# First-layer steps in four pieces, attention slots in three parts, ordered by one time table, with the sinks a slot later

## The chip, the core and the metric

The kernel runs on one core of a Trainium2 chip. The core has a matrix engine (PE, with its weight loads listed as PEld), a vector engine (DVE), a scalar engine (ACT), a general engine (POOL) and a queue engine that only issues transfers (SP). Each takes its instructions in the order in which they were put down for it, and they wait for one another through semaphores. The metric is the device time of one execution in microseconds.

## The reference

Sliding-window attention with sink columns, over 4 batches of 8 heads, 768 positions and 64 dimensions, is followed by a two-layer network over its 3072 rows of 512 values. Of the reference this is what matters:

```python
keep = is_sink | in_window            # n_sink = 4, window = 128
scores = np.where(keep, scale * (q @ k.T), -1e9)
a = np.exp(scores - max); a = a / (a.sum(-1) + 1e-9)
x = (a @ v).transpose(0, 2, 1, 3).reshape(B * S, H * D)   # 3072 x 512
h = x @ w_in                          # 512 -> 2048
g = s * np.maximum(h, 0) ** 2 + b
out = g @ w_out                       # 2048 -> 512
```

## The kernel before

**Tiling.** The 3072 rows are eight chunks of 384 (half a batch each). A chunk's attention gives its x, transposed, as two tiles `x[0]` and `x[1]` (a rounded high part and the rest, so that a product in the fast 32-bit format keeps its accuracy). The first layer of a chunk is 16 steps (`l1_steps`, line 600). A step is 12 matmuls of 128x384 into one PSUM bank `h` (line 610): eight with `x[0]`, over the four 128-row blocks of x, then four with `x[1]`. ACT then clips and stores it to a tile `g` (line 614), and SP sends two steps' result to DRAM (`gs`, line 616). After all chunks the second layer (`second_layer`) reads `gs` back, squares it and multiplies it with the second weights in 84-matmul units (line 727). It takes the last third of the time and the change doesn't touch it.

**Attention.** Chunks 0 and 2 (`plain_slots`) have no separate sinks. The other six use `attn_slots` (line 422): a chunk is 24 units (eight heads, three blocks of 128 queries), and a unit passes through stages some slots apart.

- `unit_a` (line 314): two matmuls give the scores `sc` in a PSUM bank, DVE masks them and takes their maximum (line 331, `negm`), ACT takes the exponential `sm` (337), POOL copies the sink columns to `psk` (339).
- `unit_b`, LB = 3 slots later: PE transposes `sm` into a bank `tp` (350, 351), ACT rounds it to `hl` (355), DVE subtracts for the low part (356).
- `unit_c`, LC = 5 slots after the first: PE multiplies with the values into a bank `o` (389). At a head's last block ACT and DVE move it out (397, 398). At every fourth head PE transposes `psk` into `ts` (402), ACT and DVE make `xsk` of it (404, 405).
- `unit_d`, LD = 1 slot later, at every fourth head: for two pairs of heads PE multiplies `xsk` into `os` and `zb` (414, 416), DVE adds and scales (417, 418), ACT and POOL write the pair's `x[0]` and `x[1]` (419, 420).

Loads and the splitting of queries, keys and values (`load_pair`, `load_keys`, `load_sinks`, `prep_head`, on SP, ACT, DVE and POOL) stand some slots ahead in the table `ahead`, but never ahead of the chunk's own first slot.

**Banks.** PSUM has eight banks here: five in a pool `psA` for `sc`, `tp` and `o`, three in a pool `psO` for `h`, `ts`, `os` and `zb`.

**What sets the order.** The main loop (lines 943 to 972) writes a first-layer step of the chunk before, then as many attention slots as are due by a simple ratio: 210 slots over 112 steps, two steps ahead. So one or two whole slots follow each whole step. Each attention chunk has 24 slots that start a unit and 6 in which the last units run out; the next chunk's first slot comes behind these. Into the slots the making of second-layer weights is strewn (`early_w2`, 30 tasks, with DVE operations of up to 128x1024 at lines 227, 228 and 635). The framework then orders each engine's instructions by this order and by when it thinks that they can run.

Of the kernel before, what the change touches and what calls it, by code (L numbers as in the profile page):

```python
# [15 lines left out]
P = 128  # L16
B, H, S, D = 4, 8, 768, 64
NS = 8
BLK = 3
# [17 lines left out]
NT = B * S // TB  # L37
E0, LB0, LC0 = 9, 6, 8
ORDER = 0, 2, 1, 3, 4, 5, 6, 7
LB, LC, LD, L2, LEAD = 3, 5, 1, 2, 2  # L40


@with_exitstack
def tile_kernel(ctx, tc, qT, kT, k0, v, vsk, n_sink, window, w1, w2, s, b, out):
# [362 lines left out]
    def unit_d(k, h, i):  # L407

        if h % 4 == 3 and i == BLK - 1:
            xs = k.pairs[h // 2].xs  # L410
            for pr in (h // 2 - 1, h // 2):
                pp = k.pairs[pr]
                os_ = po("os")
                nc.tensor.matmul(os_[:, :CH], pp.vs, xs, start=True, stop=True)
                zb = po("zb")
                nc.tensor.matmul(zb[:, :CH], sels[pr % 2], xs, start=True, stop=True)
                nc.vector.tensor_tensor(out=pp.x, in0=os_[:, :CH], in1=pp.x, op=ALU.add)
                nc.vector.tensor_tensor(out=pp.x, in0=zb[:, :CH], in1=pp.x, op=ALU.mult)
                nc.scalar.copy(k.x[0][:, pr, :], pp.x)
                nc.gpsimd.tensor_tensor(out=k.x[1][:, pr, :], in0=pp.x, in1=k.x[0][:, pr, :].bitcast(F32), op=ALU.subtract)  # L420

    def attn_slots(c):
        k = new_chunk(c)
        units, ahead = [], {}
        for pr in range(H // 2):
            h, t0 = 2 * pr, 2 * BLK * pr
            units += [(h + hh, i) for hh in range(2) for i in range(BLK)]
            todo = ((-5, load_pair, pr), (-5, load_keys, h), (-2, load_sinks, pr), (-2, prep_head, h), (-2, load_keys, h + 1),
                    (1, prep_head, h + 1))
            for d, fn, a in todo:  # L430
                ahead.setdefault(max(t0 + d, 0), []).append((fn, a))
        n = len(units)

        def slot(t):
            def f():
                if t == 0:
                    make_x(k)
                for fn, a in ahead.get(t, ()):
                    fn(k, a)
                if t < n:  # L440
                    unit_a(k, *units[t])
                if 0 <= t - LB < n:
                    unit_b(k, *units[t - LB])
                if 0 <= t - LC < n:
                    unit_c(k, *units[t - LC])
                if 0 <= t - LC - LD < n:
                    unit_d(k, *units[t - LC - LD])
            return f

        return k, [slot(t) for t in range(n + LC + LD)]  # L450

    def plain_slots(c):
        k = Chunk()
# [144 lines left out]
    def l1_steps(k, before):  # L600

        tk = slice(k.c * CH, (k.c + 1) * CH)
        g = {}

        def l1(f):
            before(f)
            h = po("h")
            order = [(cc, wi, 0) for cc in range(NCC) for wi in range(2)] + [(cc, 0, 1) for cc in range(NCC)]
            for i, (cc, wi, xi) in enumerate(order):
                nc.tensor.matmul(h[:, :CH], w_in(f, wi)[:, cc * P:(cc + 1) * P], k.x[xi][:, cc, :],  # L610
                                 start=(i == 0), stop=(i == len(order) - 1))
            if f % 2 == 0:
                g[0] = kept.tile([P, 2, CH], F32, tag="g", name="g", bufs=3)
            nc.scalar.activation(g[0][:, f % 2], h[:, :CH], AF.Relu, scale=1.0 / WUP)  # L614
            if f % 2 == 1:
                nc.sync.dma_start(gs[f // 2][:, :, tk], g[0])

        return [lambda f=f: l1(f) for f in range(NF)]

    wc, raw2, T2 = {}, {}, {}  # L620
    spilled = {q: dram.tile([P, 7, 2, HD], F32R, tag=f"wd{q}", name=f"wd{q}") for q in range(EARLY, EARLY + SPILL)}
# [323 lines left out]
            weights(NP - 1, (i - 20) // 2)  # L945
    first_cm.__exit__(None, None, None)
    early = early_w2()
    n_early, n_plain, done = 5 * (EARLY + SPILL), 0, 0
    steps, slots = [], []
    for j in range(NC_):  # L950
        steps += l1_steps(k, before if j == 0 else lambda f: None)
        if j + 1 < NC_:
            k, more = (plain_slots if j == 0 else attn_slots)(ORDER[j + 1])
            slots += more
            n_plain = n_plain or len(more)
    n_last = len(steps) - NF
    i = 0
    for n in range(n_last):
        steps[n]()
        while i < len(slots) and i * n_last < (n + 1 + LEAD) * len(slots):  # L960
            slots[i]()
            i += 1
            if i == n_plain:
                scalars()
            if i > n_plain and done < n_early and (i - n_plain) * (n_early + 1) >= (done + 1) * (len(slots) - n_plain):
                next(early)()
                done += 1
        if i == len(slots):
            break
    wk_cm.__exit__(None, None, None)  # L970

    p2_cm = tc.tile_pool(name="p2", bufs=1)
# [4 lines left out]
    for m in range(n + 1, len(steps)):  # L977
        steps[m]()
        m -= n_last
# [64 lines left out]
```

## Time and profile before

| | us |
|---|---|
| median of 3 runs | 762.31 (761.02 to 762.97) |
| the profiled execution | 757.87 |
| its span, first to last instruction | 756.1 |
| first step of the first layer begins | 30.5 |
| first attention unit with sinks begins | 105.1 |
| last sinks | 461.1 |
| second layer begins | 503.5 |

The profiled execution is one run, 4.4 us below the median of the others; 1.8 us of it lie outside the span. In the profile a busy PE is not a PE at its peak, since the ends of matmuls are modelled; what counts is the start of one to the start of the next, and the idle time that the waits list.

### The profile page before, as it was taken

The numbers are of one execution on the slowest core, as the hardware profiler recorded it, in microseconds if no ns is written. First come the engines' busy times: TensorE is split into PE (matmuls) and PEld (weight loads), VectorE is DVE, ScalarE is ACT, GpSimd is POOL, SyncE is SP. The second block draws the span as 40 slices with busy tenths as digits, with TensorE's granted clock in tenths as the row PEclk, the third lists the DMA queues.
The fourth block names the chain that finished last, engine by engine and source line by source line (L and its number), as shares of the span: only waits on it lengthen the run. The fifth ranks groups of instructions, "written<-read, shape, count | busy, mean of one in ns | idle before, by whom it ended". The sixth has DMA issues, their size and how long they took to land. (4 is left out here: it accounts for less than half of the span.)

```text
span 756.1 us, 14225 instructions
## 1 busy us (share of the span) xinstructions
PE 708.1 (94%) x4852; PEld 673.9 (89%) x4852; DVE 552.2 (73%) x1367; ACT 543.1 (72%) x1253; POOL 225.3 (30%) x377
## 2 busy tenths in 40 slices
PE   8889999889899999899989989989999999999995
PEld 4678799889889899899889889989999999999995
DVE  7865655875686786795685883558888989798883
ACT  5989878768877888787887873556766576666661
POOL 4232344645544554555445551110000000000000
PEclk9999999999999999999999999999999999999998
DMA  8932254365455456354354324963353534453421
GB/s 206 374 120 85 63 179 121 117 192 205 124 164 211 132 190 209 124 169 128 101 195 129 111 71 171 331 241 113 112 150 108 163 112 142 115 164 112 151 74 60
DMA packets 63312, 114.12 MB, mean 151 GB/s; under 512 B 11520, under 2 KB 38784, under 8 KB 60416
## 3 DMA queue, kind: packets, MB, share of 16 engines
q1 hardware_dynamic: 61712, 107.43, 44.4%
q0 software_dynamic: 432, 5.51, 2.2%
q8 instruction: 40, 0.66, 0.3%
q14 instruction: 40, 0.33, 0.2%
q10 hardware_dynamic: 1088, 0.20, 0.1%
HBM read 76.16 MB, written 36.96 MB: 150 GB/s over the span
## 5 line engine op out<-in xcount | busy, mean ns | idle before, releaser
L610 PE MATMUL h<-x,w 128*128 128x384 f32 x1536 | 299.2, 343 | 3.7 <-ACT g L614 2.6
L610 PEld LDWEIGHTS h<-x,w 128*128 128x128 f32 x1536 | 265.5, 190 | 6.7 <-ACT g L614 3.8
L727 PE MATMUL Q<-v,gH 128*128 128x256 f32 x1008 | 127.8, 283 | 0.0
L727 PEld LDWEIGHTS Q<-v,gH 128*128 128x128 f32 x1008 | 124.0, 192 | 0.0
L727 PE MATMUL Q<-v,gA 128*128 128x256 f32 x756 | 99.0, 283 | 1.5 <-DVE gA L709 1.5
L698 ACT ACTIVATE gs<-gs,sbu 128x1024 f32<-128x1024 f32 x48 | 55.2, 1151 | 62.3 <-DMA gs<-gs 58.4
L727 PEld LDWEIGHTS Q<-v,gA 128*128 128x128 f32 x756 | 94.3, 192 | 1.8 <-DVE gA L709 1.7
L614 ACT ACTIVATE g<-h 128x384 f32<-128x384 f32 x128 | 62.5, 489 | 42.7 <-PE h L610 33.1
L337 ACT ACTIVATE sm<-sm,negm 128x264 f32<-128x264 f32 (+1 forms) x144 | 72.4, 503 | 21.1 <-DVE negm L331 19.7
L356 DVE TENSOR_TENSOR hl<-tp,hl 128x256 fp32r<-128x256 f32 (+1 forms) x144 | 57.3, 402 | 29.8 <-ACT hl L355 28.2
L331 DVE CUSTOM_DVE_ANT_0 sm<-sc,msk 128x264 f32<-128x264 f32 (+1 forms) x144 | 58.2, 411 | 24.9 <-PE sc L327 22.6
L306 POOL TENSOR_TENSOR kl<-kraw,kh 128x528 fp32r<-128x528 f32 (+1 forms) x48 | 62.6, 1304 | 29.3 <-ACT kh L304 24.8
L389 PE MATMUL o<-hl,vv 128*128 128x256 f32 (+1 forms) x352 | 63.1, 296 | 5.6 <-DVE hl L356 3.5
L710 ACT CAST gH<-gs 128x1024 fp32r<-128x1024 f32 x48 | 50.0, 1042 | 19.4 <-PE Q L727 10.5
L711 DVE TENSOR_TENSOR gH<-gs,gH 128x1024 fp32r<-128x1024 f32 x48 | 58.5, 1219 | 6.5 <-ACT gH L710 6.5
L708 ACT ACTIVATE gA<-gs,sbu 128x512 fp32r<-128x512 f32 x96 | 53.7, 607 | 9.5 <-PE Q L727 9.5
L339 POOL COPY psk<-sm 128x24 f32<-128x24 f32 x144 | 34.1, 241 | 86.8 <-ACT sm L337 79.6
L389 PEld LDWEIGHTS o<-hl,vv 128*128 128x128 f32 x352 | 48.6, 192 | 9.0 <-DVE hl L356 4.0
L709 DVE SCALAR_TENSOR_TENSOR gA<-gs,sbu,gA 128x512 fp32r<-128x512 f32 x96 | 54.9, 612 | 0.2 <-ACT gA L708 0.2
L355 ACT CAST hl<-tp 128x256 fp32r<-128x256 f32 (+1 forms) x144 | 49.7, 352 | 1.1 <-PE tp L351 0.6
L700 DVE SCALAR_TENSOR_TENSOR gs<-gs,sbu 128x256 f32<-128x256 f32 x48 | 23.2, 483 | 35.8 <-ACT gs L698 34.4
L326 PE MATMUL sc<-kh,qs 128*128 128x264 f32 (+1 forms) x144 | 42.0, 294 | 2.6 <-DVE negm L331 2.0
(180 smaller groups left out, 1214.4 us busy)
## 6 DMA issues: line engine op xcount, KB each, us to landing
gs<-g SPq DMA_DIRECT2D x64, 384.0 KB, 3.3
gs<-gs SPq DMA_DIRECT2D x48, 512.0 KB, 4.1
kraw<-in_kT SPq DMA_DIRECT2D x32, 264.0 KB, 2.8
wraw<-in_w SPq DMA_DIRECT2D x8, 1024.0 KB, 10.0
vraw<-in_w SPq DMA_DIRECT2D x6, 1024.0 KB, 5.3
out<-ot SPq DMA_DIRECT2D x12, 512.0 KB, 3.6
wd<-v SPq DMA_DIRECT2D x3, 1792.0 KB, 6.8
v<-wd POOLq DMA_DIRECT2D x3, 1792.0 KB, 8.9
```

Of the source, the lines that this page charges most:

```text
L306: nc.gpsimd.tensor_tensor(out=hd.kl[:, :kw], in0=hd.k[:, :kw], in1=hd.kh[:, :kw].bitcast(F32), op=ALU.subtract)
L331: nc.vector.tensor_tensor_reduce(out=sm[:, :n], in0=sc[:, :n], in1=m, scale=-0.125, scalar=BIG, op0=ALU.add, op1=ALU.min, accum_out=negm[: ...
L337: nc.scalar.activation(sm[:, :n], sm[:, :n], AF.Exp, bias=negm[:, uu], scale=-1.0, accum_out=pp.zz[:, i, hh:hh + 1])
L356: nc.vector.tensor_tensor(out=lo, in0=tp[:, a:z], in1=hi.bitcast(F32), op=ALU.subtract)
L389: nc.tensor.matmul(hd.o[:, q0:q0 + n * P], hd.vv[:, kb, :], hd.hl[:, t, c0 * P:(c0 + n) * P], start=(hd.n == 0), stop=(i == BLK - 1 and kb ...
L610: nc.tensor.matmul(h[:, :CH], w_in(f, wi)[:, cc * P:(cc + 1) * P], k.x[xi][:, cc, :], start=(i == 0), stop=(i == len(order) - 1))
L614: nc.scalar.activation(g[0][:, f % 2], h[:, :CH], AF.Relu, scale=1.0 / WUP)
L698: nc.scalar.activation(g[:, 0], g[:, 0], AF.Square, scale=root_ap)
L708: nc.scalar.activation(o[:, :, 0], x, AF.Identity, bias=b1_ap, scale=1.0)
L709: stt(out=o[:, :, 1], in0=x, scalar=b1_ap, in1=o[:, :, 0].bitcast(F32), op0=ALU.add, op1=ALU.subtract)
L711: nc.vector.tensor_tensor(out=H[:, :, 1], in0=S, in1=H[:, :, 0].bitcast(F32), op=ALU.subtract)
L727: nc.tensor.matmul(Q[j][:, rb], left[j][:, gi, rb * P:(rb + 1) * P], right[j][:, wi], start=(q == 0 and rb == 0 and i == 0), stop=(last an ...
```

## The change

A first-layer step is cut in four pieces of three matmuls (`PIECES = 4`); the bank `h` is opened by the first piece, and ACT reads it after the last. An attention slot is cut in three parts: `unit_a` with the loads and preparations, `unit_b`, and `unit_c` with `unit_d`. The six attention chunks form one row of 144 units, so that the units of one chunk follow those of the chunk before with no slots in between to run out, and loads stand ahead across the border of chunks. `LD` is 2 in place of 1. The x tiles are allocated at a chunk's first sinks and not at its first slot. The merging goes by a list of times, in steps: the plain chunk's slots end by step 14, row t of the attention stands at t2 + t dt, with t2 = 24 x 14/30 = 11.2 and dt = (112 - 2 - 11.2)/151 = 0.654 of a step, its three parts a third of dt apart; the weight tasks are spread evenly from step 16 to 110.

```diff
-LB, LC, LD, L2, LEAD = 3, 5, 1, 2, 2
+LB, LC, LD, L2, LEAD, PIECES = 3, 5, 2, 2, 2, 4
...
-    def attn_slots(c):
-        k = new_chunk(c)
+    def attn_slots(chunks):
...
+        for k in chunks:
+            for pr in range(H // 2):
+                h, t0 = 2 * pr, len(units)
+                units += [(k, h + hh, i) for hh in range(2) for i in range(BLK)]
...
-        def slot(t):
+        def part(t, j):
             def f():
...
+                if j == 0:
+                    for fn, k, a in ahead.get(t, ()):
+                        fn(k, a)
+                for fn, lag, of in ((unit_a, 0, 0), (unit_b, LB, 1), (unit_c, LC, 2), (unit_d, LC + LD, 2)):
+                    if of == j and 0 <= t - lag < n:
+                        fn(*units[t - lag])
             return f
...
+        return [[part(t, j) for j in range(3)] for t in range(n + LC + LD)]
...
-        def l1(f):
-            before(f)
-            h = po("h")
-            order = [(cc, wi, 0) for cc in range(NCC) for wi in range(2)] + [(cc, 0, 1) for cc in range(NCC)]
-            for i, (cc, wi, xi) in enumerate(order):
+        order = [(cc, wi, 0) for cc in range(NCC) for wi in range(2)] + [(cc, 0, 1) for cc in range(NCC)]
+        n = len(order) // PIECES
+
+        def l1(f, piece):
+            if piece == 0:
+                before(f)
+                g["h"] = po("h")
+            h = g["h"]
+            for i, (cc, wi, xi) in list(enumerate(order))[piece * n:(piece + 1) * n]:
                 nc.tensor.matmul(h[:, :CH], w_in(f, wi)[:, cc * P:(cc + 1) * P], k.x[xi][:, cc, :],
                                  start=(i == 0), stop=(i == len(order) - 1))
+            if piece < PIECES - 1:
+                return
...
+    chunks = [k, k2] + [new_chunk(c) for c in ORDER[2:]]
+    rows = attn_slots(chunks[2:])
+    steps = [f for j, c in enumerate(chunks) for f in l1_steps(c, before if j == 0 else lambda f: None)]
+    n_last = (NC_ - 1) * NF
+
+    t1 = (NF - LEAD) / len(plain)
+    t2 = H * BLK * t1
+    dt = (n_last - LEAD - t2) / len(rows)
+    todo = [(t * t1, f) for t, f in enumerate(plain)] + [(t2, scalars)]
+    todo += [(t2 + (t + j / 3) * dt, f) for t, row in enumerate(rows) for j, f in enumerate(row)]
+    todo += [(NF + (t + 0.5) * (n_last - LEAD - NF) / n_early, lambda: next(early)()) for t in range(n_early)]
+    todo.sort(key=lambda x: x[0])
+    n = 0
+    while todo:
+        while todo and todo[0][0] * PIECES < n + 1:
+            todo.pop(0)[1]()
         steps[n]()
+        n += 1
```

**Place 1: PE in the middle of attention.** This is PE's order in the first attention chunk before: the end of a slot, a second slot, then a whole step (`x_2` is the x of chunk 2, `w` the first weights).

```order
L350 MATMUL tp<-identr,sm 128x128
L351 MATMUL tp<-identr,sm 128x128
L389 MATMUL o<-hl,vv 128x128 x2
L389 MATMUL o<-hl,vv 128x256 x2
L326 MATMUL sc<-kh,qs 128x264
L327 MATMUL sc<-kl,qs 128x264
L350 MATMUL tp<-identr,sm 128x128
L351 MATMUL tp<-identr,sm 128x128
L610 MATMUL h<-x_2_543,w_524 128x384 x8
L610 MATMUL h<-x_2_544,w_524 128x384 x4
L326 MATMUL sc<-kh,qs 128x264
```

And this is PE's order in the same chunk now.

```order
L610 MATMUL h<-x_2_524,w_504 128x384 x3
L326 MATMUL sc<-kh,qs 128x264
L327 MATMUL sc<-kl,qs 128x264
L610 MATMUL h<-x_2_524,w_504 128x384 x2
L610 MATMUL h<-x_2_525,w_504 128x384
L350 MATMUL tp<-identr,sm 128x128
L351 MATMUL tp<-identr,sm 128x128
L610 MATMUL h<-x_2_525,w_504 128x384 x3
L389 MATMUL o<-hl,vv 128x128 x2
L389 MATMUL o<-hl,vv 128x256 x2
L610 MATMUL h<-x_2_524,w_546 128x384 x3
```

Three matmuls of the first layer now stand between scores, transposes and products, where twelve stood behind two whole slots.

**Place 2: PE from the sinks' transposes to the sinks' products.** Before, at the end of the chunk's first half:

```order
L402 MATMUL ts<-identr,psk_102 128x128 x3
L610 MATMUL h<-x_2_543,w_665 128x384 x8
L610 MATMUL h<-x_2_544,w_665 128x384 x4
L326 MATMUL sc<-kh,qs 128x264
L327 MATMUL sc<-kl,qs 128x264
L350 MATMUL tp<-identr,sm 128x128
L351 MATMUL tp<-identr,sm 128x128
L414 MATMUL os<-xsk,vs 128x384
```

Now, at the same heads, from the second piece on (a piece of three and one pair of scores stand between `ts` and these rows):

```order
L610 MATMUL h<-x_2_524,w_631 128x384 x3
L350 MATMUL tp<-identr,sm 128x128
L351 MATMUL tp<-identr,sm 128x128
L610 MATMUL h<-x_2_524,w_631 128x384 x2
L610 MATMUL h<-x_2_525,w_631 128x384
L326 MATMUL sc<-kh,qs 128x264
L327 MATMUL sc<-kl,qs 128x264
L610 MATMUL h<-x_2_525,w_631 128x384 x3
L350 MATMUL tp<-identr,sm 128x128
L351 MATMUL tp<-identr,sm 128x128
L610 MATMUL h<-x_2_524,w_631 128x384 x3
L389 MATMUL o<-hl,vv 128x256 x2
```

The product of the sinks follows two matmuls later. Between the transposes and it there are 15 matmuls of the first layer, two pairs of scores, two pairs of transposes and four products, where there were 12, one pair and one pair.

**Place 3: PE at the first border of attention chunks.** These rows are the chunk's last sinks now, up to the first matmul of the next chunk's first layer (its x is `x_1`).

```order
L416 MATMUL os<-xsk,vs 128x384
L418 MATMUL zb<-xsk,sel_100 128x384
...
L416 MATMUL os<-xsk,vs 128x384
...
L418 MATMUL zb<-xsk,sel_101 128x384
L610 MATMUL h<-x_2_525,w_1032 128x384
L389 MATMUL o<-hl,vv 128x128 x2
L389 MATMUL o<-hl,vv 128x256 x2
L610 MATMUL h<-x_2_525,w_1032 128x384 x3
L326 MATMUL sc<-kh,qs 128x264
L327 MATMUL sc<-kl,qs 128x264
L610 MATMUL h<-x_1_1738,w_470 128x384 x3
```

Before, two whole steps stood between these sinks and that matmul; now it is the rest of one.

## Rows read from the trace of the kernel before

**Rows 1.** The page, its first part: busy time, share of the span and instructions of each engine.

```profile
PE 708.1 (94%) x4852; PEld 673.9 (89%) x4852; DVE 552.2 (73%) x1367; ACT 543.1 (72%) x1253; POOL 225.3 (30%) x377
```

**Rows 2.** Busy time in three stretches (attention beside the first layer; the rest of the first layer; the second layer): length, then busy us and count of PE, PEld, DVE, ACT and POOL, the granted clock, the DMA share and GB/s.

```profile
105.00:462.00 357.00, 333.17 (x2140) 321.25 (x2138) 261.17 (x756) 285.46 (x800) 179.60 (x311) 0.99 0.46 147
462.00:503.00 41.00, 38.18 (x214) 36.99 (x215) 20.05 (x36) 22.43 (x37) 7.54 (x7) 1.00 0.76 264
503.00:757.00 254.00, 243.00 (x2020) 242.45 (x2018) 202.86 (x362) 149.27 (x191) 0.00 (x0) 0.99 0.41 128
```

**Rows 3.** Waits of PE from 105 to 462 us, all of them: who waited for whom, us in total, times, the longest.

```profile
PE tp L350 <- DVE hl L356: 7.7, 9, 1.8
PE os L414 <- DVE xsk L405: 6.8, 5, 2.4
PE o L389 <- DVE hl L356: 3.5, 6, 1.6
PE sc L326 <- DVE negm L331: 2.0, 3, 0.8
PE o L389 <- DVE xm L398: 0.9, 1, 0.9
PE sc L326 <- DVE xm L398: 0.6, 2, 0.4
PE o L389 <- ACT hl L355: 0.5, 1, 0.5
PE os L414 <- ACT g L614: 0.3, 2, 0.2
PE o L389 <- DVE negm L331: 0.2, 1, 0.2
```

**Rows 4.** The chain that ended last, one attention slot and the first-layer step behind it, where PE ran without a wait: start us, us, what.

```profile
447.83 0.17 PE sc L326
448.00 0.12 PE sc L327
448.13 0.11 PE tp L350
448.24 0.11 PE tp L351
448.35 0.47 PE o L389 x4
448.81 2.11 PE h L610 x12
```

**Rows 5.** PE in order of time around the first sinks: start us, us, then the instructions, and in brackets the idle time ahead of them and what ended it.

```profile
134.09 0.49 PE L402 MATMUL ts<-identr,psk 128*128 128x128 f32 x3
134.34 2.34 PE L610 MATMUL h<-x,w 128*128 128x384 f32 x12
...
139.53 0.44 PE L414 MATMUL os<-xsk,vs 128*128 128x384 f32 x1 [2.39 <-DVE xsk L405]
```

**Rows 6.** PE from 310 to 321 us, in the same form: a step, the longest wait on VectorE, and the step behind it.

```profile
310.67 2.34 PE L610 MATMUL h<-x,w 128*128 128x384 f32 x12
...
313.89 0.28 PE L327 MATMUL sc<-kl,qs 128*128 128x264 f32 x1
315.98 0.33 PE L350 MATMUL tp<-identr,sm 128*128 128x128 f32 x1 [1.80 <-DVE hl L356]
...
317.65 3.23 PE L610 MATMUL h<-x,w 128*128 128x384 f32 x12
```

**Rows 7.** One us behind that wait, in the columns of rows 2; the granted clock is the number ahead of the last two.

```profile
317.00:318.00 1.00, 1.00 (x6) 1.00 (x6) 0.42 (x1) 0.98 (x5) 0.38 (x2) 0.50 0.32 59
```

**Rows 8.** DVE in the same stretch.

```profile
310.28 2.03 DVE L228 SCALAR_TENSOR_TENSOR vraw<-vraw,vt 128x1024 int32<-128x1024 int32 x1
...
313.15 2.31 DVE L305 TENSOR_TENSOR qs<-qraw,qs 64x384 fp32r<-64x384 f32 x1
315.50 0.42 DVE L356 TENSOR_TENSOR hl<-tp,hl 128x256 fp32r<-128x256 f32 x1
```

**Rows 9.** POOL in the same stretch.

```profile
313.16 1.89 POOL L230 TENSOR_TENSOR vraw<-vraw 128x1024 int32<-128x1024 int32 x1
```

**Rows 10.** All instructions of line 305 on DVE: shortest, median and longest in ns, first and last start in us.

```profile
L305 DVE TENSOR_TENSOR qs<-qraw,qs x48: 551/554/2314, 97.7 to 441.6; 64x384 fp32r<-64x384 f32 x48
```

**Rows 11.** The sinks of one half chunk and what they hand to the first layer, all engines, in order of time.

```profile
226.44 0.34 PE L414 MATMUL os<-xsk,vs 128*128 128x384 f32 x1
...
227.44 1.02 DVE L417 TENSOR_TENSOR xm<-os,xm 128x384 f32<-128x384 f32 x2
...
228.38 1.01 DVE L418 TENSOR_TENSOR xm<-zb,xm 128x384 f32<-128x384 f32 x2
...
229.50 0.92 ACT L419 CAST x<-xm 128x384 fp32r<-128x384 f32 x2
...
230.34 2.29 POOL L420 TENSOR_TENSOR x<-xm,x 128x384 fp32r<-128x384 f32 x2
```

**Rows 12.** Waits of PE from 40 to 105 us, the one that counts.

```profile
PE tp L549 <- ACT sm_p L537: 4.5, 4, 2.0
```

**Rows 13.** A part of that stretch, in the columns of rows 2.

```profile
60.00:80.00 20.00, 19.52 (x107) 16.47 (x107) 11.95 (x29) 19.49 (x51) 5.76 (x8) 1.00 0.30 87
```

**Rows 14.** Waits of ACT from 105 to 462 us, the one on a load.

```profile
ACT kh L304 <- DMA kraw<-in_kT: 6.2, 7, 1.6
```

More of the change, by code (lines that the diff above doesn't have):

```diff
@@ L410, in unit_d @@
             xs = k.pairs[h // 2].xs
+            if h == 3:
+                make_x(k)
             for pr in (h // 2 - 1, h // 2):
@@ L420, in unit_d @@
                 nc.gpsimd.tensor_tensor(out=k.x[1][:, pr, :], in0=pp.x, in1=k.x[0][:, pr, :].bitcast(F32), op=ALU.subtract)
-    def attn_slots(c):
-        k = new_chunk(c)
+    def attn_slots(chunks):
         units, ahead = [], {}
[L425 to L431, printed above, removed]
+        for k in chunks:
+            for pr in range(H // 2):
+                h, t0 = 2 * pr, len(units)
+                units += [(k, h + hh, i) for hh in range(2) for i in range(BLK)]
+                todo = ((-5, load_pair, pr), (-5, load_keys, h), (-2, load_sinks, pr), (-2, prep_head, h), (-2, load_keys, h + 1),
+                        (1, prep_head, h + 1))
+                for d, fn, a in todo:
+                    ahead.setdefault(max(t0 + d, 0), []).append((fn, k, a))
         n = len(units)
-        def slot(t):
+        def part(t, j):
             def f():
[L436 to L447, printed above, removed]
+                if j == 0:
[4 more added lines that the diff above has]
+                        fn(*units[t - lag])
             return f
-        return k, [slot(t) for t in range(n + LC + LD)]
+        return [[part(t, j) for j in range(3)] for t in range(n + LC + LD)]
     def plain_slots(c):
@@ L603, in l1_steps @@
         g = {}
[L605 to L609 removed]
+        order = [(cc, wi, 0) for cc in range(NCC) for wi in range(2)] + [(cc, 0, 1) for cc in range(NCC)]
[6 more added lines that the diff above has]
+            for i, (cc, wi, xi) in list(enumerate(order))[piece * n:(piece + 1) * n]:
                 nc.tensor.matmul(h[:, :CH], w_in(f, wi)[:, cc * P:(cc + 1) * P], k.x[xi][:, cc, :],
                                  start=(i == 0), stop=(i == len(order) - 1))
+            if piece < PIECES - 1:
+                return
             if f % 2 == 0:
[L613 to L614 removed]
+                g["r"] = kept.tile([P, 2, CH], F32, tag="g", name="g", bufs=3)
+            nc.scalar.activation(g["r"][:, f % 2], h[:, :CH], AF.Relu, scale=1.0 / WUP)
             if f % 2 == 1:
[L616 to L618 removed]
+                nc.sync.dma_start(gs[f // 2][:, :, tk], g["r"])
+        return [lambda f=f, piece=piece: l1(f, piece) for f in range(NF) for piece in range(PIECES)]
     wc, raw2, T2 = {}, {}, {}
@@ L947, in tile_kernel @@
     early = early_w2()
[L948 to L958, printed above, removed]
-        steps[n]()
[L960 to L969, printed above, removed]
+    n_early = 5 * (EARLY + SPILL)
+    k2, plain = plain_slots(ORDER[1])
+    chunks = [k, k2] + [new_chunk(c) for c in ORDER[2:]]
[13 more added lines that the diff above has]
+            todo.pop(0)[1]()
+        steps[n]()
+        n += 1
     wk_cm.__exit__(None, None, None)
@@ L976, in tile_kernel @@
     todo = todo[:4] + [lambda: reload(EARLY + 1)] + todo[4:] + [lambda: reload(EARLY + 2)]
-    for m in range(n + 1, len(steps)):
+    for m in range(n, len(steps)):
         steps[m]()
-        m -= n_last
+        if m % PIECES < PIECES - 1:
+            continue
+        m = m // PIECES - n_last
         if m == NF // 2:
```

## Prediction

> **What bounds the kernel now.** I read the engines' shares first. PE is busy for 94% of the span, no other engine for more than 73% [rows 1], so the time is PE's work plus what PE idles. The split by stretches says where idle time is left. In the second layer PE is busy for 243.0 of 254 us, in the rest of the first layer for 38.2 of 41; while attention runs beside the first layer it is busy for 333.2 of 357, so some 24 us are idle there [rows 2]. The change leaves the second layer alone and removes no matmul. It can therefore give what PE idles between 105 and 462 us, a little before that, and nothing else.
>
> The waits name the idle time [rows 3]. 6.8 us in five waits are sinks: `os` waits for DVE's `xsk`. The rest, but for 0.3 us on ACT's reading of `h`, is 15.4 us in 23 waits, and in these PE wants a PSUM bank or an `hl` which DVE has not come to yet (0.5 us: ACT). No wait is for a load. So a late DVE is what holds PE in this stretch, not a full one: it is busy for 261 of 357 us, ACT for 285 [rows 2].
>
> Why it is late shows at the longest such wait. A weight operation of 2.03 us and one splitting a query, of 2.31 us, stand on DVE ahead of the `hl` that PE wants [rows 8], and PE, with all its banks out, idles 1.80 us [rows 6]. The query's splitting usually takes 0.554 us and here 2.31 [rows 8, 10]; POOL runs a 1.89 us addition in the same two microseconds [rows 9].
>
> A wait costs more than its idle time. From 313.89 to 315.98 us are 2.09; the next matmul would have started 0.12 after [rows 4], so 1.97 are lost for 1.80 listed, 0.17 more [rows 6]. 28 waits make 4.8 us of this. And behind that wait PE's granted clock stood at half, 1.2 in place of 2.4 GHz [rows 7], and the step took 3.23 us where one takes 2.34 [rows 6]. Over the whole stretch the mean clock is 0.99 [rows 2]; a hundredth of 357 us is 3.6 us, an estimate, as the row is rounded.
>
> **The change part by part.**
>
> *Pieces and thirds.* Before, two slots take 2 x 0.98 us of PE and the step behind them 2.11 [rows 4]: 4.07 us per two units. Now 151 rows share 98.8 steps, 1.53 to a step, so two units come with 1.31 steps: 1.96 + 2.76 = 4.72 us. DVE and ACT get 0.65 us more for the same two units, since the empty slots at the ends of chunks are gone. The other half of the effect is the spacing: four or five banks were asked for within 1.96 us and none in the next 2.11; now they are asked for evenly over 4.72, against the same five banks. By these numbers, an estimate, a lag of DVE of little over 2 us could be met by a burst; now it has to last some 4 us before PE runs out of banks. The 23 waits are 0.67 us each on average, about the 0.65 gained. Taken from each, it leaves only the long ones, three of which are known (1.8, 1.6 and 0.9): 1.15 + 0.95 + 0.25 = 2.35, and some for the rest of the nine and six. Since another order also brings DVE's long operations to new places, I leave twice that and a bit, 5.4 us, and take 10 us of the 15.4 as gained. Bounds: all 15.4, or nothing (first rival).
>
> *Sinks a slot later.* Between `ts` and `os` PE had a step, a pair of scores and a pair of transposes: 2.11 + 0.24 + 0.22 = 2.57 us; where that was not enough, it waited up to 2.39 more [rows 5]. By the new order there are 15/12 of 2.11, two pairs of each, and four products: 2.64 + 0.48 + 0.44 + 0.47 = 4.03 us. 1.46 us more leave 0.9 of the longest wait and little of the other four, which are 1.1 us on average. I leave 1.3 and take 5.5 us. Bounds 4 and 6.8.
>
> *What comes with each wait.* If about 20 of 28 waits go, 20 x 0.17 = 3.4 us. Of the clock's 3.6 us I take half, 1.8, since only some waits are followed by a lower clock: no row says which. Bounds 0 and 8.4 for both.
>
> *x tiles closer to their use.* The last sinks of a chunk are put down 30.67 x 0.654 = 20.1 steps after t2 = 11.2, so at 31.3, where the next first layer begins at 32; before there were two whole steps. From `os` to the last low part of x it took 226.44 to 232.63, 6.2 us [rows 11]. By the new order PE has 3.5 us of work from that `os` to the next chunk's first matmul and 5.9 to the twelfth, which needs that last part (counted in the durations of rows 4). So PE waits 0.3 us, or more where POOL is late with its 2 x 1.14 us. Each later border has 0.3 of a step more, about a microsecond. I take 1.5 us in all; bounds 0 and 6 (three borders at 2 us).
>
> *`h` holds its bank longer.* A step opens a bank for its whole length, 2.11 + 1.53 x 0.98 = 3.6 us in place of 2.11, out of three, and the sinks take four in a row from the same three. Before, this showed in two waits of 0.3 us [rows 3]. I take 0.2 us for each of the twelve groups of sinks, 2.4 us. From above it is bounded by the time in which sinks hold banks, 226.44 to 229.39 [rows 11], 2.95 us x 12 = 35; from below by 0.
>
> *At nothing.* The queue of SP: loads of a chunk's first heads now stand five rows ahead of the border, past the stores of `gs`; PE waits for no load, and ACT's 6.2 us of waiting for keys [rows 14] cost PE nothing by rows 3. Without that cover, one load would cost the 1.6 us of the longest. The plain chunk's slots come a seventh faster and attention starts two steps earlier, in a stretch where ACT is nearly full (19.49 of 20 us [rows 13]) and PE has lost 4.5 us to it [rows 12]: it may lose that again, or lose nothing, and I take no change; bounds -4.5 and +4.5. The order of waiting at pieces: a part that waits now has a third of a step behind it, which PE can't take out of turn; 1 us. The rest of the first layer and the second layer begin earlier by what is gained, as their loads wait for `gs`, which comes earlier too.
>
> Sum: 10 + 5.5 + 3.4 + 1.8 = 20.7 us gained, 1.5 + 2.4 + 1 = 4.9 paid: 15.8 us. The sum is made in an execution of 757.87 us, 4.4 below the median; the waits are the same work in either, so I take it from the median: 762.3 - 15.8 = 746.5 us.
>
> **The rivals.**
>
> *The lag of DVE stays (757).* The long DVE operations are long because POOL works at the same time [rows 8, 9], and the 48 splittings run from 551 to 2314 ns [rows 10]. The change removes none of these operations on either engine. If each lag is several microseconds, 0.65 more don't help, and PE waits as long in total as before, at other places. Then only the sinks are won: 5.5, five tails of 0.17, less 1.5 at the borders: 4.9 us, 757.4. Against it: most of the 23 waits are short. The Trainium skill has this as a rule (GPSIMD Engine Reference, Specifications): GpSimd's SBUF interfaces are shared with VectorE, which contend when a VectorE instruction has two SBUF inputs or uses a two-port mode. By that rule, the trace agrees: the slow splitting has two SBUF inputs and stood beside POOL for the whole of its 2.31 us.
>
> *Slower: sinks and `h` meet in three banks (768).* If the next step's first piece always finds the three banks taken by the open step's reading and by `os` and `zb`, PE stands until DVE has freed them, and everything behind the piece stands with it. The price is up to 2.95 us at each of twelve groups; at 2.2 us it is 26 us against 20.7 - 2.5 gained: 762.3 + 8 = 770, at 2 us 768. It decides from 1.7 us per group on. For it: `h` is open 70% longer. Against it: rows 3 show 0.3 us from the same pool, and the order puts pieces between the four products.
>
> *Borders (752).* The x tiles come late at the first three borders, at the bound of 6 us and more where POOL has the keys of the next chunk in front: 15.8 - 5 = 11 us gained, 751.5.
>
> *All of it (735).* Every wait goes with its tail and clock, at no price: 22.2 + 4.8 + 3.6 = 30.6 us less 3 for the borders: 735.
>
> That the pieces are put together again by the framework's ordering is no rival: the built order shows them apart.
>
> **How the numbers follow.** Forecast 50%, DVE's lag stays 21%, borders 13%, all of it 7%, slower by the banks 9%. The range takes in the first three and half of the fourth: 737 to 760 us. A measurement here tells about 0.3% (2.3 us) from no change. Faster by more than that: all of the forecast and the borders, all of it, and five sixths of the first rival, 0.87; the rest of that rival is within it, with a little of the banks at half price, 0.05; slower 0.08.
>
> **What would show it.** In the profile of the changed kernel, PE's waits between 100 and 450 us should fall from 22 us to about 8, `os` for `xsk` from 6.8 to about 1, DVE releases from 15 to about 5; the mean clock there should round to 1.00. A step begun behind sinks should not wait for `h` by more than 0.2 us. The first matmul with each new chunk's x may wait up to a microsecond for line 420's POOL copy at the first border only. I am wrong if waits on DVE stay near 15 us (then lag, not bursts, is the cause), if a wait of `h` on DVE's lines 417 and 418 stands high in the list, or if the plain stretch grows by more than what attention gains.

## The result and the profile after

The changed kernel takes 765.25 us (median of 8, 763.49 to 767.04), the kernel before, on the same chip, 761.99. The ratio is 1.0058, with a 95% interval of 1.0036 to 1.0081: some 4 us slower, where 16 faster were forecast. The profiled execution took 767.04 us, and its span is 765.3.

The page's first part for the kernel after (against [rows 1]):

```profile
PE 711.9 (93%) x4852; PEld 674.2 (88%) x4852; DVE 559.1 (73%) x1367; ACT 543.2 (71%) x1253; POOL 224.9 (29%) x377
```

The same three stretches of the kernel after, moved to where its stages end (against [rows 2]; the number behind POOL's is the granted clock):

```profile
105.00:462.00 357.00, 330.25 (x2112) 315.10 (x2111) 260.46 (x722) 281.16 (x794) 179.32 (x310) 0.98 0.46 146
462.00:510.00 48.00, 45.25 (x259) 43.52 (x258) 23.49 (x41) 25.95 (x43) 7.59 (x7) 1.00 0.66 234
510.00:765.00 255.00, 244.84 (x2021) 244.09 (x2019) 203.30 (x362) 149.66 (x191) 0.00 (x0) 0.98 0.41 128
```

The loss is where the gain was to be. From 105 to 462 us PE does 28 matmuls fewer than before and the clock is a hundredth lower, so 7 us more of the first layer are left behind it (48 in place of 41). PE's waits in that stretch, all of them (against [rows 3]; lines 416 to 422 and 616 were 414 to 420 and 614):

```profile
PE os L416 <- DVE xm L419: 7.4, 7, 1.5
PE zb L418 <- ACT g L616: 6.5, 6, 2.1
PE os L416 <- ACT g L616: 5.5, 3, 2.4
PE tp L350 <- DVE hl L356: 3.5, 7, 0.8
PE o L389 <- DVE xm L398: 1.1, 2, 0.6
PE sc L327 <- POOL kl L306: 0.9, 1, 0.9
PE zb L418 <- DVE xm L419: 0.7, 1, 0.7
PE zb L418 <- DVE xm L420: 0.3, 1, 0.3
```

Two things came as forecast: no `os` waits for `xsk` any more (6.8 us before), and the waits in the pool of five fell from 15.4 to 4.6 us. But 20.4 us now stand at `os` and `zb`, which wait for a bank of the pool of three until ACT has read `h` or DVE has added: 1.7 us in each of the twelve groups of sinks.

The waits also cost clock. PE in order of time at one of them, and the granted clock behind it:

```profile
350.16 0.34 PE L416 MATMUL os<-xsk,vs 128*128 128x384 f32 x1
352.57 0.44 PE L418 MATMUL zb<-xsk,sel 128*128 128x384 f32 x1 [2.07 <-ACT g L616]
352.85 0.97 PE L610 MATMUL h<-x,w 128*128 128x384 f32 x3
```
```profile
353.20:356.40 3.20, 3.20 (x12) 3.11 (x12) 2.40 (x7) 0.84 (x4) 2.06 (x5) 0.50 0.79 253
```

There are five such stretches at half clock between 98 and 475 us, and a sixth at 523.7, behind a wait of 1.51 us in the second layer; the kernel before had two. Each is some 3.4 us long and so costs about 1.7. The two profiled executions show more of this than the others: their mean clocks are 0.983 and 0.991, and their spans lie 9.2 us apart where the medians lie 3.3 apart. Over all executions the mean clock is 0.985 in the kernel after and, in the rounds of the experiments, 0.988 to 0.990 in the kernel before, which is worth 2 to 4 us.

This looks as if the rival "sinks and `h` meet in three banks" had come true. The engines behind PE tell another story. First the kernel before, waits of ACT and of DVE from 120 to 460 us:

```profile
ACT g L614 <- PE h L610: 21.8, 28, 2.6
ACT sm L337 <- DVE negm L331: 17.7, 22, 2.3
```
```profile
DVE hl L356 <- ACT hl L355: 25.9, 29, 2.9
```

And the kernel after, the same stretch:

```profile
ACT sm L337 <- DVE negm L331: 38.7, 46, 2.2
...
ACT g L616 <- PE h L610: 1.8, 3, 0.8
```
```profile
DVE hl L356 <- ACT hl L355: 44.5, 55, 1.7
```

Before, ACT was often done with everything and waited for PE to finish `h`. Now it almost never is; instead ACT's exponential waits for DVE's `negm`, and DVE's subtraction `hl` for ACT's copy, 83.2 us together in place of 43.6.

### The profile page after: what moved, and what is told of

Read it like the earlier page. It is cut to its first block, busy times and chain, and to the rows that moved or that the text cites. A ratio compares the mean times of both kernels' runs of the same rounds, so it can differ in the third digit from the quotient of the medians.

```text
span 765.3 us, 14216 instructions
## 1 busy us (share of the span) xinstructions
PE 711.9 (93%) x4852; PEld 674.2 (88%) x4852; DVE 559.1 (73%) x1367; ACT 543.2 (71%) x1253; POOL 224.9 (29%) x377
## 4 chain that ended last, share of the span: by engine, by line
PE 56%; ACT 14%; DVE 10%; DMA 6%; issue 4%; POOL 4%; SPq 0%; ACTq 0%; POOLq 0%; DVEq 0%
PE Q L729 30%; PE h L610 16%; DMA gs<-gs 3%; PE o L389 3%; DMA kraw<-in_kT 2%; ACT sm L337 2%; ACT g L616 2%; POOL kl L306 2%; DVE hl L356 1%; DVE qs L305 1%; DVE sm L331 1%; ACT hl L355 1%; ACT y L397 1%; PE sc L327 1%; PE tp L351 1%
## 5 line engine op out<-in xcount | busy, mean ns | idle before, releaser
L610 PE MATMUL h<-x,w 128*128 128x384 f32 x1536 | 348.1, 352 | 3.4 <-ACT g L616 2.6
L610 PEld LDWEIGHTS h<-x,w 128*128 128x128 f32 x1536 | 257.4, 192 | 6.6 <-ACT g L616 3.9
L339 POOL COPY psk<-sm 128x24 f32<-128x24 f32 x144 | 37.3, 263 | 93.4 <-ACT sm L337 87.9
L389 PE MATMUL o<-hl,vv 128*128 128x256 f32 (+1 forms) x352 | 58.1, 280 | 1.6 <-DVE xm L398 1.1
L389 PEld LDWEIGHTS o<-hl,vv 128*128 128x128 f32 x352 | 54.0, 192 | 3.7 <-DVE xm L398 1.9
L305 DVE TENSOR_TENSOR qs<-qraw,qs 64x384 fp32r<-64x384 f32 x48 | 41.9, 872 | 11.0 <-ACT qs L301 9.9
```

The lines of the kernel that those rows point to most:

```text
L389: nc.tensor.matmul(hd.o[:, q0:q0 + n * P], hd.vv[:, kb, :], hd.hl[:, t, c0 * P:(c0 + n) * P], start=(hd.n == 0), stop=(i == BLK - 1 and kb ...
```

## The experiments

Each ran in five rounds against the kernel before on its chip. Ratios are to that kernel, with 95% intervals; "mutual waits" are the two rows just shown added up (`sm` for `negm` on ACT, `hl` for `hl` on DVE, 120 to 460 us).

| kernel | us | ratio | mutual waits, us |
|---|---|---|---|
| after | 765.25 | 1.0058 [1.0036, 1.0081] | 83.2 |
| e1 four and four banks | 768.11 | 1.0111 [1.0075, 1.0148] | 84.3 |
| e2 whole steps | 753.28 | 0.9921 [0.9893, 0.9949] | 53.1 |
| e3 sinks early | 765.52 | 1.0081 [1.0051, 1.0111] | 99.6 |
| e4 before, sinks late | 763.99 | 1.0071 [1.0044, 1.0098] | 45.4 |
| e5 sinks between steps | 771.68 | 1.0136 [1.0091, 1.0182] | 92.7 |
| e6 sinks in other pool | 765.85 | 1.0088 [1.0053, 1.0123] | 87.0 |
| e7 pairs apart | 765.50 | 1.0073 [1.0047, 1.0099] | 79.8 |
| e8 whole, pairs apart | 754.21 | 0.9927 [0.9902, 0.9952] | 61.5 |
| e9 exponential behind copy | 763.60 | 1.0076 [1.0053, 1.0100] | 77.2 |
| e10 whole, the same | 756.09 | 0.9960 [0.9939, 0.9982] | 49.6 |
| e11 before, the same | 757.52 | 0.9988 [0.9963, 1.0013] | 39.1 |
| e12 two pieces | 755.30 | 0.9951 [0.9926, 0.9975] | 60.7 |
| e13 no turns | 752.69 | 0.9907 [0.9879, 0.9935] | 42.2 |
| e14 no turns, pairs apart | 750.44 | 0.9871 [0.9844, 0.9897] | 43.9 |
| e15 whole, no turns | 757.10 | 0.9958 [0.9940, 0.9976] | 37.2 |
| e16 one late cut | 757.19 | 0.9970 [0.9949, 0.9990] | 56.7 |
| e17 before, no turns | 755.76 | 0.9967 [0.9942, 0.9992] | 40.8 |
| e18 no turns, other pool | 747.15 | 0.9838 [0.9806, 0.9871] | 46.9 |

**First: is it the open bank?** Four runs undo one part each.

```diff
 e1:
-    psA = ... bufs=5     psO = ... bufs=3
+    psA = ... bufs=4     psO = ... bufs=4
 e2:
-LB, LC, LD, L2, LEAD, PIECES = 3, 5, 2, 2, 2, 4
+LB, LC, LD, L2, LEAD, PIECES = 3, 5, 2, 2, 2, 1
 e3:
+LB, LC, LD, L2, LEAD, PIECES = 3, 5, 1, 2, 2, 4
 e4 (the kernel before):
-LB, LC, LD, L2, LEAD = 3, 5, 1, 2, 2
+LB, LC, LD, L2, LEAD = 3, 5, 2, 2, 2
```

> The changed kernel with the banks divided four and four (one taken from the pool of sc, tp and o for the pool of h, ts, os and zb). In the changed kernel's profile PE waits 20.4 us at the sinks for a bank (for ACT's reading of h, lines 616, or for DVE's line 419), and six stretches at half clock follow waits. Bank theory (h holds a bank over its whole step, so that three are too few for the sinks): these waits fall below 5 us, the clock rises to 0.99, and even if the waits for sc, tp and o grow by 5 to 10 us from now 8, the time falls to 748 to 757 us. ACT theory (ACT comes to the reading of h 2 to 4 us late because of the finer order, whatever the banks): PE only meets the same lag a little later, at the next step's bank or at psA; sinks' and other waits together stay above 20 us and the time at 761 to 766.

> The changed kernel with steps in one piece (PIECES = 1): one row of units, three parts and the later sinks stay. Bank theory: no step is open while the sinks run, so the waits of os and zb for ACT's reading of h fall from 12.0 us to below 2 and the time to 752 to 758; waits for DVE's releases (sc, tp, o) come back up from 8 us toward the 15.4 of before. ACT theory: ACT has the same work in nearly the same order, os and zb go on waiting for line 616 by 8 us or more, and the time stays at 762 or more.

> The changed kernel with LD = 1, the sinks a slot earlier as before. Bank theory: a step is open at the sinks all the same, so 15 us or more of waiting for banks stay, and waits for xsk come on top by 1 to 7 us: 764 to 770 us. If it is the place of the sinks (two slots later they fall on a worse point of ACT's order) that costs: the bank waits fall by half and the time to 755 to 760.

> The kernel before with LD = 2 alone. By my sum the sinks a slot later are worth 5.5 us where no step is open at them: waits of os for xsk fall from 6.8 us to about 1 and the time to 755 to 758. If the later place itself brings waits for banks or later x tiles, it stays at 760 to 764.

The pieces are the fault: whole steps under the same time table run 5 us faster than the kernel before. So the time table, the one row and the late sinks are together worth something, and the cut costs 1.4% (1.0058 against 0.9921), some 10 us. The times of e2 and e3 are those that the bank theory gave, but in e2 `os` still waits 5.6 us for ACT's reading of `h`, where under 2 were expected. e1 was slower than both theories had it: a fourth bank for `h` and the sinks gave nothing, and part of the waits moved to scores, which then had four (`sc` for `hl`, 7.0 us). The surprise is e4: sinks a slot later, alone, make the kernel before slower. Three of PE's waits in e4 (98 to 475 us):

```profile
PE zb L416 <- DVE xm L417: 4.7, 5, 1.6
...
PE os L414 <- ACT g L614: 2.3, 4, 1.0
...
PE os L414 <- DVE xsk L405: 0.3, 1, 0.3
```

`xsk` is in time (0.3 in place of 6.8 us), and PE waits 7.0 us at the very next steps of the same sinks instead. The late sinks take nothing off; they change what is waited for. From 105 to 462 us PE's waits add up to 23.4 us (22.5 before). The stretches at half clock add up to 17.1 us in this one execution (6.8 before); over all executions of that round the mean clock is 0.986 in e4 and 0.988 in the kernel before, which is some 1.5 of the 5 us that e4 is slower. The rest is not explained.

**Second: other banks for the sinks, or fewer at a time.**

```diff
 e5 (unit_d as a fourth part, at the nearest end of a step):
+    todo += [(int(t2 + (t + 2 / 3) * dt + 0.5), row[3]) for t, row in enumerate(rows)]
 e6:
-                os_ = po("os") ... zb = po("zb")
+                os_ = ps("os") ... zb = ps("zb")
 e7, and with PIECES = 1 e8 (the second pair of heads a slot behind the first):
-            for pr in (h // 2 - 1, h // 2):
+            for pr in (h // 2 - 1 + second,):
...
+                                    (lambda *u: unit_d(*u, 1), LC + LD + 1, 2)):
```

> The kernel after, but sinks are put down only where one step of the first layer has ended and the next has not begun, so that no `h` is half written while `os` and `zb` want banks. Open-bank theory: PE's waits of `os` and `zb` for banks fall from 20 us to the 10.5 us that the kernel with whole steps had, half-clock stretches from five to two or three, and the time to 752-757 us. Pieces theory (the cutting of steps itself, or the places that DVE's long operations get, is what costs): 762-768 us as the kernel after.

> The kernel after, but `os` and `zb` take their banks from the pool of five that scores, transposes and products use, instead of the pool of three that `h` is in. Open-bank theory: `os` and `zb` no longer wait for ACT's reading of `h`; half or more of the 20 us goes, some comes back as waits of scores and transposes; 748-758 us. Lag theory (DVE is late whoever asks, and more banks only change who waits, as four and four banks at 768 suggest): the waits return in full under `sc`, `tp` and `o`, 762-769 us.

> The kernel after, but a group of sinks is cut in two: the second pair's `os` and `zb` come a slot behind the first pair's, so that two banks are asked for at a time and not four. Open-bank theory: waits of `os` and `zb` fall from 20 us to 6 or less, since a whole slot passes before the second pair wants the banks that DVE's first addition releases: 747-756 us. Lag theory: DVE's additions stand behind its other work as before and PE waits elsewhere for them, 760-767 us.

> Whole steps (PIECES = 1, which ran at 753.3 us), and the two pairs of sinks a slot apart. Open-bank theory: of the 10.5 us that `os` and `zb` still wait there, 7 or more go, and the time is 743-749 us, under both kernels. Lag theory: 751-756 us, as with whole steps alone.

All four missed what the bank theory said. With four pieces the time stays at 765 or worse, wherever the sinks get their banks (e5, at 771.7, is slower than either theory had it). PE's longest waits from 105 to 462 us in e6, where `os` and `zb` no longer share the pool of three with `h`:

```profile
PE zb L418 <- DVE hl L356: 12.6, 15, 1.8
PE tp L350 <- DVE hl L356: 5.6, 8, 1.8
```

And in e7:

```profile
PE zb L418 <- ACT g L617: 10.4, 8, 2.7
PE h L611 <- ACT g L617: 6.4, 5, 2.1
```

In all PE waits 24.2 us there in e6 and 27.0 in e7, as in the kernel after (25.9), under other names. So PE waits for ACT and DVE, whoever of its tiles is in front, and the open bank was mainly the place where their lateness came out.

**Third: why are ACT and DVE late?** ACT from 227 us in the kernel after, in order of time:

```profile
227.15 0.36 ACT L355 CAST hl<-tp 128x256 fp32r<-128x256 f32 x1
228.22 0.41 ACT L337 ACTIVATE sm<-sm,negm 128x136 f32<-128x136 f32 x1 [0.71 <-DVE negm L331]
...
228.63 0.24 ACT L355 CAST hl<-tp 128x128 fp32r<-128x128 f32 x1
...
229.58 0.52 ACT L337 ACTIVATE sm<-sm,negm 128x264 f32<-128x264 f32 x1 [0.32 <-DVE negm L331]
...
230.09 0.35 ACT L355 CAST hl<-tp 128x256 fp32r<-128x256 f32 x1
```

DVE in the same stretch:

```profile
227.54 0.42 DVE L356 TENSOR_TENSOR hl<-tp,hl 128x256 fp32r<-128x256 f32 x1
227.89 0.29 DVE L331 CUSTOM_DVE_ANT_0 sm<-sc,msk 128x136 f32<-128x136 f32 x1
...
228.90 0.29 DVE L356 TENSOR_TENSOR hl<-tp,hl 128x128 fp32r<-128x128 f32 x1 [0.72 <-ACT hl L355]
229.11 0.42 DVE L331 CUSTOM_DVE_ANT_0 sm<-sc,msk 128x264 f32<-128x264 f32 x1
...
230.47 0.42 DVE L356 TENSOR_TENSOR hl<-tp,hl 128x256 fp32r<-128x256 f32 x1 [0.93 <-ACT hl L355]
```

They take turns. ACT copies `hl`; DVE subtracts; behind that, on DVE, stands the reduction of another unit's scores; behind its `negm`, on ACT, the exponential; behind that the next copy. Four instructions of two engines run one after the other, and each engine idles while the other works. If DVE had the reduction ahead of the subtraction, copy and reduction would run side by side, and then subtraction and exponential. In the built order of the instructions it can be counted for how many of the 144 units an exponential and the reduction it needs stand behind the same copy's two halves: 48 before, 71 after, 40 with whole steps.

```diff
 e9 (and with PIECES = 1 e10; the same edit in the kernel before e11):
     the exponential and psk leave unit_a for a new unit_e
+                for fn, lag, of in ((unit_a, 0, 0), (unit_b, LB, 1), (unit_e, 0, 1), (unit_c, LC, 2), ...
 e12:
+LB, LC, LD, L2, LEAD, PIECES = 3, 5, 2, 2, 2, 2
```

> The kernel after, but a unit's exponential is written behind the other unit's transposes and their copy, instead of before them: nothing else, and each step of the first layer is still in four pieces. Turn-taking theory: on ACT an exponential stands behind the copy `hl`, on DVE the scores' reduction behind the subtraction `hl`; where both belong to the same copy, DVE waits for ACT and ACT then for DVE, one after the other. By the built order that is so for 48 of 144 units in the kernel before, 71 in the kernel after, 40 with whole steps, and 44 here. So ACT's waits for `negm` from 120 to 460 us fall from 38.7 us to about 25, PE's waits by 10 or more, and the time to 751-758 us. Bank theory, or any cost of the pieces themselves: 763-768 us, as the kernel after.

> Whole steps (753.3 us) and the exponential behind the copy: 22 of 144 units take turns in place of 40. Turn-taking theory: ACT's waits for `negm` from 23.0 us to about 15, and 745-751 us. Bank theory: the places of `h`, `os` and `zb` are as before, 752-755 us.

> The kernel before with that one edit: 20 of 144 units take turns in place of 48. Turn-taking theory: under the kernel before by 5 us or more, 750-756 us. If the turns cost only where steps are in pieces, or not at all: 758-762 us.

> The kernel after with steps in two pieces: 58 of 144 units take turns, between the 40 of whole steps and the 71 of four pieces. Turn-taking theory: 757-762 us, between 753.3 and 765.3. Bank theory says much the same, since `h` is open for half as many pieces; a jump to 765 would say that any cut costs in full.

All four missed. e9 had 44 turns by the count, but on the chip the mutual waits fell only from 83.2 to 77.2 us, and the time hardly: the count in the built order does not say what the queues do when they run. e10 and e11 gained nothing that can be told from e2 and from the kernel before. e12 came out better than forecast (755.3, where 757 was the least), at the level of whole steps. The theory was left untested, as the suspected wait had not been taken away.

**Fourth: the turns taken away.** e13 adds edges that set an order and no wait: `behind` puts an instruction after the last one of the named kind on its own engine, the exponential after the copy (`hi`) and the subtraction after the reduction (`negm`).

```diff
 e13 (on e9; with the edit of e7 e14; with PIECES = 1 e15; in the kernel before e17):
+    def behind(ins, key):
...
+        ex = nc.scalar.activation(sm[:, :n], sm[:, :n], AF.Exp, ...)
+        if "hi" in last:
+            behind(ex, "hi")
...
+        behind(nc.vector.tensor_tensor(out=lo, in0=tp[:, a:z], in1=hi.bitcast(F32), op=ALU.subtract), "negm")
 e16 (PIECES = 2, nine and three matmuls):
+        cut = 0, 9, len(order)
...
```

> The kernel after, four pieces, with two kinds of edges that set order only: an exponential stands behind the last copy `hl` on ACT, and a subtraction `hl` behind the last reduction of scores on DVE. By the built order 3 of 144 units take turns, in place of 71. Turn-taking as the cause: ACT's waits for `negm` and DVE's for `hl`, 38.7 and 44.5 us from 120 to 460 us, fall to 50 or less together, and the time to 750-757 us. Turn-taking as a symptom (ACT and DVE are late for another reason): 762-767 us, whatever these waits do.

> As the run before it, and the two pairs of sinks a slot apart. If the banks and the turns are two limits that each hide the other, the run before it stays above 758 and this one comes to 748-755 us. If neither is the cause: 762-767 us. If turns alone are the cause: about the time of the run before it.

> Whole steps with the same edges: 3 of 144 units take turns in place of 40. Turn-taking as the cause: 745-751 us, under the 753.3 of whole steps. As a symptom: 752-757 us.

> The kernel after with steps in two pieces of nine and three matmuls; attention's parts stand between them by the same time table. By the built order 45 of 144 units take turns, fewer than with two equal pieces (58; 755.3 us). Late reading of `h` (ACT comes to `h` late because parts stand just ahead of the last short piece): 760 us or more, and ACT's reading releases PE for as long as with four pieces (12 us). Number of cuts, or turns by built order: 752-757 us.

e13 is the kernel after with four pieces, thirds, late sinks and its banks, and it takes 752.7 us. ACT's and DVE's waits in it:

```profile
ACT sm L349 <- DVE negm L337: 14.5, 20, 1.9
...
ACT g L630 <- PE h L624: 9.2, 11, 2.1
```
```profile
DVE hl L370 <- ACT hl L369: 27.7, 44, 2.2
```

The mutual waits are halved and ACT again waits for PE's `h`. The same instructions as above, on ACT in e13, take 2.25 us from copy to copy in place of 2.94:

```profile
223.01 0.37 ACT L369 CAST hl<-tp 128x256 fp32r<-128x256 f32 x1
223.26 0.53 ACT L349 ACTIVATE sm<-sm,negm 128x264 f32<-128x264 f32 x1
...
223.77 0.26 ACT L369 CAST hl<-tp 128x128 fp32r<-128x128 f32 x1
224.49 0.41 ACT L349 ACTIVATE sm<-sm,negm 128x136 f32<-128x136 f32 x1 [0.45 <-DVE negm L337]
...
225.26 0.37 ACT L369 CAST hl<-tp 128x256 fp32r<-128x256 f32 x1
```

PE's waits from 105 to 462 us fall from 25.9 to 19.8 us and the half-clock stretches between 98 and 475 from five to three: 6.1 + 2 x 1.7 = 9.5 of the 12.5 us by which the way from the first `sc` to the last `h` is shorter (412.0 to 399.5 us); the other 3 are not accounted for. The stretch in the second layer is gone too. At `os` and `zb` 15.2 us are left of 20.4, though no bank was touched. These are the longest:

```profile
PE os L430 <- DVE xm L433: 7.2, 7, 1.9
PE zb L432 <- ACT g L630: 3.8, 6, 1.0
PE os L430 <- ACT g L630: 3.6, 3, 1.6
```

With the pairs apart as well (e14) the time is 750.4 us, and there is one half-clock stretch in all ahead of the last few us; the intervals of e13 and e14 overlap.

e15 missed: with whole steps the same edges give no gain (757.1 against 753.3), though the mutual waits fall to 37.2. There ACT waits for PE's `h` 22.6 us; that an engine with so much time in hand loses none by a turn is a reading that fits, and no run tests it. e16 speaks against the late short piece and does not rule it out: by that rival 760 us or more, measured 757.2, but `os` still waits 9.8 us for ACT's reading of `h`, where 12 were expected by it.

**Last: what the edges do without the pieces, and the other pool again.**

```diff
 e17: the edges of e13 in the kernel before
 e18 (on e14):
+                os_ = ps("os") ... zb = ps("zb")
```

> The kernel before with the same edges: by the built order 17 of 144 units take turns, in place of 48. In the kernel before ACT and DVE wait for each other 17.7 + 25.9 us, about what is left with four pieces and the edges (14.5 + 27.7), so the turns hardly hold it: 755-761 us, level with the kernel before. If the edges are worth 10 us anywhere: 748-752 us.

> Four pieces with the edges and the pairs apart (750.4 us), and `os` and `zb` in the pool of five. If the banks of the pool of three are the next limit: the 13 us of waits of `h` and `zb` go, half of them come back on scores and transposes, 742-748 us. If PE has only moved on to the next late release: 748-754 us.

e17 is level with or a little under the kernel before, as expected; the edges take hardly anything off the mutual waits there (40.8 of 43.6 us, in an execution that was the slowest of its twelve). e18 is the fastest of all, 1.6% under the kernel before. It is 3 us under e14, but their intervals overlap, and PE's waits from 105 to 462 us are no fewer (17.9 us against 15.9). The intervals of e13 and e18, the two edits for the sinks' banks together, do not overlap, while each of these edits gave nothing with the turns in place (e6 1.0088, e7 1.0073). e18's longest waits:

```profile
PE tp L364 <- DVE hl L370: 5.8, 10, 1.8
PE zb L432 <- DVE hl L370: 5.0, 6, 1.4
```

## Why the prediction was wrong, point by point

- **The bound** held. PE's waits between 105 and 462 us sort the kernels: 15.9 to 19.9 us in those at 0.997 or under, 21.3 to 28.6 in all others, with e17 the one exception (22.9). What they were put down to, a late DVE, was half of it: ACT's and DVE's own waits were not read beyond one row [rows 14], and they would have shown that these two wait for each other 43.6 us in the kernel before.
- **Pieces and thirds, 10 us gained:** this is the step that failed. The waits that it counts did fall, from 15.4 to 4.6 us, but PE's waits in all rose from 22.5 to 25.9, since more came up at `os` and `zb`. The step took the time in which ACT and DVE finish a unit as given, and reckoned that "DVE and ACT get 0.65 us more for the same two units". But asked for one tile at a time, in the order that the framework then built, they waited for each other 83.2 us in place of 43.6. Four pieces cost 1.4% against whole steps (e2), and edges that part the turns give 1.5% back with the pieces still in place (e13). The Trainium skill (TensorE: Matmul & The Clock Gate, Architectural detail) says that ACT and DVE queues are strictly first in, first out. By that rule, the traces agree: in the rows of the third experiment the 128x128 copy at 228.63 has had its `tp` since 226.1 (PE's transpose of 225.80), and it stands while ACT idles 0.71 us, until the exponential ahead of it has its `negm`.
- **Sinks a slot later, 5.5 us:** the wait for `xsk` went, as forecast, and the time did not. Alone the edit costs 0.7% (e4), and taking it back in the kernel after changes nothing (e3). PE meets the late engines a matmul further on (in e4 4.7 us for DVE's `xm` and 2.3 for ACT's `g`). Why e4 is 5 us slower, with mutual waits as before (45.4), is not settled.
- **`h` holds its bank longer, 2.4 us:** 20.4 us of waits stand at this place, 1.7 in each group, at which the rival "sinks and `h` meet in three banks" was to decide, and its 768 us is nearest to what was measured. That the rival's number came out is luck: its mechanism is not the cause of the loss, as other banks and fewer at a time left the time at 765 or above (e5 to e7). The term itself was mis-sized, 2.4 us for 20.4. With the turns gone, all that was done for the sinks' banks is worth some 5.5 us (752.7 to 747.2, e13 to e18). That the banks are a second limit, behind the turns, fits this; PE's waits fall only from 19.8 to 17.9 us with it, and the mean clock rises from 0.989 to 0.993, some 3 us.
- **Tails and clock, 5.2 us gained:** of the wrong sign with the waits. Three more half-clock stretches beside attention and one in the second layer cost 4 x 1.7 = 6.8 us in the two profiled executions, and 2 to 4 over all of them.
- **x tiles, 1.5 us:** not paid; no wait of PE names line 422.
- **The plain stretch, no change within 4.5:** at the start of attention `sc` now waits 1.9 us for `qs` and 0.5 for `kl`, within the bounds.
- **The rival "the lag of DVE stays"** had the outcome of e5 to e7 right, PE waiting as long at other places. Its ground, POOL and DVE in each other's way, was not tried apart. It does not tell the slow kernels from the fast: the 46 splittings of queries from 105 to 462 us average 751 ns before and 886 after, but 846 in e13 and 914 in e18, the fastest.

What is shown: with four pieces, the order of ACT's and DVE's instructions makes the loss, since edges that change this order alone take it away (e13 against e9, which has all but the edges: 0.9907 against 1.0076). All four-piece kernels with 77 to 100 us of mutual waits are slower than the kernel before, and the three with 42 to 47 are faster. What is not shown:

- That mutual waits cost time in general. Whole steps (53.1 us) and two pieces (60.7) have more of them than the kernel before (43.6) and are faster, and taking them down gained nothing in e15.
- Which of the two kinds of edges does it, the exponential behind the copy or the subtraction behind the reduction; they were not tried apart.
- Why evenly spaced pieces bring ACT and DVE into turns on the chip and two pieces or whole steps do so less. That ACT has less time in hand fits the rows (its waits for `h`: 1.8 us with four pieces, 6.7 with two, 17.2 with whole steps), but e9 shows that the count of turns in the built order does not foretell it.
- A gain of four pieces over whole steps. With the edges they are level (e13 0.9907, e2 0.9921), and e18's edits for the banks were not tried together with whole steps and edges.

## What to carry to other kernels

When PE waits on two engines that work in a chain, read what these wait for before spacing PE's work out: if they wait for each other, finer interleaving can make it worse, and an order edge between two of their instructions may be worth more than banks. Their waits alone do not say what a kernel will take, though: they cost where neither engine has time in hand, as it seems here. If a wait goes to a new name at the same length when what it named is removed (`xsk` to `xm`, `h` to `hl`), the cause lies elsewhere. And an edit that gave nothing is worth another try once the limit in front of it is gone: pairs apart and the other pool gave nothing with the turns (e6, e7), and together 5 us without them (e13 to e18).

## What the runs showed of the hardware that was not expected

- Cutting steps is neutral for PE itself. From start to start, the first matmul of a piece takes 43 ns more than the others' 174 (mean of 319 in the kernel after), which is some 9 us more than with whole steps; and the short matmuls between pieces take less: `sc` 125 ns in place of 140, `o` of 128 columns 91 in place of 102. Added up over the matmuls from the first `sc` to the last `h`, waits and half clock taken out, it is some 368 to 369 us with four pieces, with two and with whole steps.
- In the kernel after, five of the six stretches at half clock began within 1.6 us of the end of a wait of 0.7 to 2.4 us (2.41 ahead of the one at 206.3, 1.41 at 264.3, 2.07 at 353.1, 0.72 with 1.69 shortly before it at 414.5, 1.51 at 523.7). Its fastest execution has the highest mean clock and its slowest the lowest: 763.49 us at 0.988, 767.04 at 0.983. e14 and e18, the two fastest, have one such stretch each ahead of the last few us.
